# Zeros first, some loads on another queue, and all instruction orders searched anew: recurrent attention and squared-ReLU layers on one core

## The chip, the cores and the metric

The kernel runs on one core of one Trainium2 chip. The metric is the device time of one execution in microseconds (us). The engines are TensorE (PE; its weight loads are listed as PEld), VectorE (DVE), ScalarE (ACT), GpSimd (POOL) and SyncE (SP), which only issues DMAs here. POOL issues DMAs as well, on a queue of its own. In the profile's rows SPq stands for SP as it issues.

## The reference

```python
def _attn_ref(q, k, v, alpha):            # batch 4, heads 8, sequence 768, head size 48, float32
    for t in range(S):
        state = alpha[:, :, t, :, None] * state + np.einsum('bhd,bhe->bhde', k[:, :, t], v[:, :, t])
        y[:, :, t] = np.einsum('bhd,bhde->bhe', q[:, :, t], state)

def _moe_ref(x, w_in, w_out):             # x: 3072 x 384, w_in: 384 x 2048, w_out: 2048 x 384
    h = x @ w_in
    r = np.maximum(h, 0.0)
    return (r * r) @ w_out
```

x is y with batch and sequence as rows and all heads side by side as columns. The inputs are float32; the kernel computes its matmuls in bfloat16.

## The kernel before, in words

The sequence is cut into 12 units of 256 tokens (3 stretches of 768 by 4 batches; `units`). A unit g goes through five stages:

- **Loads** (`load`, L529): alpha, k, q, v of the unit: `lda3`, `ldk3`, `ldq3`, `ldv3` for unit 3. Unit 0 and those from 3 on go through SP's queue. Units 1 and 2 and the weights (`win0` to `win2`, `wout0`, `wout1`, function `weight`, L503) go through POOL's queue, in the order of the list `QUEUE` (L389). A table `AFTER` (L1095) makes a load wait until another has landed: win1 waits for k0, a2 for win1, wout0 for win2, wout1 for k2, the loads of unit 3 for wout0, those of unit 4 for q3.
- **Front** (`front`, L709; `front_by_heads` for unit 0, L549): logs of alpha on ACT (`ln`, `lm`), cumulative sums as matmuls with triangular matrices (`m1`, `m1i`, `m1s`), exponentials on ACT (`ei`, `ea`, `es`), products on POOL or DVE (`pr`, `bk`, `aq`), scaled keys and queries on DVE (`ekm`, `eqm`), and v as bfloat16 (`vc`). Then both are transposed: on PE for units 0 to 2 (`tr0_1` for the keys of unit 1, `tr1_1` for its queries; unit 0 has four, the second digit is the half of the heads), with an eviction after each (`et`), and by two transposing DMAs from SP for units 3 to 11 (also called `tr0_g`, `tr1_g`).
- **Scores and output** (`scores`, L904; `output`, L942): score tiles on PE (`p0_g`; unit 0 has `p0_0` and `p1_0`), masked out of PSUM by DVE (`mk0`, `mk1`), the output matmuls `y`, the state (`kv`, `sa`, `sc`, `sd`), the eviction of y (`xe`), and its transpose (`xt`): on PE for units 0 to 3, with an eviction `xv`, by a transposing DMA from SP for units 4 to 11.
- **First layer** (`first_layer`, L1008): 8 groups `s1_g_0` to `s1_g_7` of 6 matmuls each with 256 columns; each group's ReLU is `re`, its square `sq` (some squares take two groups at once).
- **Second layer** (`second_layer`, L1053): for each half of the rows 4 groups `s2_g_half_0` to `_3` of 4 matmuls each with 384 columns, an eviction `oe` and a store `out`.

Which engine issues what, and in which order, is written out by hand: the table `ORDERS` (L12) lists every operation by name for each engine. Operations without a name have a number: #1 to #13 and #16 to #19 are memsets on DVE (#19 zeroes a buffer `ZERO`, #18 is a part of a mask `OWN`, #6, #7 and #5 clear the scaled keys' and queries' buffers), #14, #15 and #20 to #22 selections on POOL that cut triangles and the identity, #23 a copy on ACT for the causal mask. The class `Program` puts each operation on the engine under which it is listed and works out its semaphore waits. Its `schedule` (L158) also works out planned starts from costs; these starts fix nothing but the order in which waits are derived and where `fill` (L236) puts filler matmuls on PE. A filler multiplies zeros by zeros into a PSUM bank that nobody reads. `fill` is called once (L1127): it puts fillers in PE's planned waits, after the memset of `ZERO` and before the first `s1` group.

In `ORDERS` the memset of `ZERO`, #19, stands last on DVE, behind `oe11_11`. `fill` therefore finds no place, and the kernel before has no filler.

Of the kernel before, what the change touches and what calls it, by code (L numbers as in the profile page):

```python
# [3 lines left out]
ALU = mybir.AluOpType  # L4
# [14 lines left out]
        sq4_7 sq4_6 re5_2 ln8 xe6 oe4_0 ei8 ea8 lm8 re5_5 re5_4 es8 sq5_5 re5_6 re5_7 re6_0 re6_1 sq5_6 ln9 re6_3 lm9
        re6_4 re6_5 ei9 ea9 es9 re6_7 re6_6 sq6_7 oe5_1 re7_1 re7_0 vc9 ln10 sq7_3 re7_5 ei10 lm10 ea10 re7_7 es10  # L20
        sq7_7 oe6_1 re8_1 sq7_5 re8_0 sq7_6 ln11 xe9 lm11 ei11 re8_4 oe7_0 re8_6 re8_5 sq8_6 ea11 re8_7 sq8_1 re9_0
        oe7_1 re9_2 es11 sq8_7 re9_4 oe8_0 xe10 sq9_1 re9_5 oe8_1 sq9_5 sq9_6 re10_1 oe9_0 oe9_1 re10_4 re10_5 re10_6
        re10_7 oe10_0 oe10_1 re11_4 sq11_5 re11_7 oe11_0 oe11_10
    """,
    "dve": """
        #7 #11 #4 #6 #5 #9 #10 #16 #12 #8 #13 #3 #1 #17 ekm0_0 ekm1_0 eqm0_0 #18 eqm1_0 et00_0 et10_0 et11_0 sa0 mk0_0
        mk1_0 ekm1 eqm1 xv0 et1_1 sc0 mk1_1 mk0_1 sa1 #2 re0_3 sq0_1 xe1 pr2 xv1 sq0_5 sc1 re1_0 re1_1 bk2 ekm2 eqm2
        re1_4 et0_2 re1_7 mk1_2 mk0_2 sa2 pr3 sc2 bk3 eqm1_3 ekm3 aq3 eqm0_3 pr4 xe2 sa3 xv2 lb4 ekm4 eqm1_4 eqm0_4
        sc3 re2_2 mk1_3 mk0_3 re2_5 sq2_5 sa4 ekm5 xv3 sc4 lb5 eqm1_5 eqm0_5 mk1_4 mk0_4 re3_2 sq3_3 sa5 re3_5 sc5
        sq3_5 bk6 ekm6 re3_6 lb6 eqm1_6 eqm0_6 mk1_5 mk0_5 re4_2 sq4_1 sa6 re4_4 re4_5 sc6 lb7 oe3_1 ekm7 eqm1_7  # L30
        eqm0_7 mk1_6 mk0_6 sd6 re5_3 sa7 sc7 sq5_3 lb8 ekm8 oe4_1 eqm1_8 eqm0_8 mk1_7 mk0_7 sq5_7 sq6_1 re6_2 xe7
        oe5_0 sa8 lb9 ekm9 eqm1_9 eqm0_9 mk1_8 mk0_8 sq7_1 pr10 re7_3 re7_2 xe8 sa9 oe6_0 re7_4 bk10 ekm10 lb10 mk0_9
        re7_6 eqm1_10 eqm0_10 mk1_9 pr11 sd7 re8_3 re8_2 sq8_3 sa10 lb11 ekm11 sq8_5 mk0_10 eqm1_11 eqm0_11 re9_1
        mk1_10 re9_3 sa11 re9_7 mk0_11 re9_6 mk1_11 re10_0 xe11 re10_2 re10_3 sq10_3 sq10_5 sq10_7 re11_0 re11_1
        re11_2 re11_3 re11_5 re11_6 sq11_6 sq11_7 oe11_11 #19
# [56 lines left out]
class Program:  # L92
# [10 lines left out]
    SWITCH = 95  # L103
# [54 lines left out]
    def schedule(self):  # L158
# [35 lines left out]
        while True:  # L194
# [5 lines left out]
            if heads and (event is None or min(heads)[0] <= event):  # L200
# [958 lines left out]
```

## Time and profile before

| | |
|---|---|
| median of 3 runs | 175.3 us (174.58 to 176.03) |
| the profiled execution | 173.93 us |
| span of its profile | 172.2 us |
| first s1 group of unit 0 starts | 18.19 us into the span |
| DMA | 33.37 MB, mean 194 GB/s |

The columns of the timeline are start, duration, engine, line, operation, out<-in, shape and count; in brackets stands how long the engine had been idle and what ended that. In the windows each engine has its busy time and number of instructions in the stretch. Durations of matmuls are modelled with their pipeline's end, so consecutive ones overlap; the distance between two starts is the pace. The tables of DMA issues give KB of one and the time from issue to landing. The chain is the work that ended last, followed back from the end.

### The profile page before, as it was taken

To read this page: it belongs to the slowest core of one execution; us is meant where nothing else is said; L and a number is where in the kernel's file an instruction comes from. 1 tells how busy PE (TensorE), PEld (TensorE's weight loads), DVE (VectorE), ACT (ScalarE), POOL (GpSimd) and SP (SyncE) were. 2 spreads that over 40 slices of the span, in tenths; PEclk is the share of its full clock that TensorE was granted. 3 is DMA by queue.
4 is the path that set the end of the run, shared out by engine and by line. 5 is a ranking of instruction groups with operands and counts; after the bars stand their busy time and mean duration, and the time that the engine had idled before them with its cause. 6 is when DMAs were issued, how large, how long until landed. Compare 5 with 4: busy or idle time off the path is not lost.

```text
span 172.2 us, 5038 instructions
## 1 busy us (share of the span) xinstructions
PE 160.9 (93%) x2200; PEld 127.6 (74%) x2200; DVE 117.2 (68%) x186; ACT 104.5 (61%) x190; POOL 64.6 (37%) x65
## 2 busy tenths in 40 slices
PE   0696999999999999999999999999999999999994
PEld 0564799756788877887877887878777877687773
DVE  4478889768977787769566848799517709355241
ACT  2837478767677866466785578377668454152240
POOL 4947214910286554481640466001012122403700
PEclk9999999999999999999999999999999999999999
DMA  5999999999997999999999999999983672220012
GB/s 139 346 256 244 291 276 212 204 272 297 159 240 183 292 221 179 221 222 251 205 221 293 219 197 243 162 286 317 183 209 115 90 84 93 48 93 0 24 71 91
DMA packets 71559, 33.37 MB, mean 194 GB/s; under 512 B 67568, under 2 KB 68592, under 8 KB 71536
## 3 DMA queue, kind: packets, MB, share of 16 engines
q1 hardware_dynamic: 69024, 26.75, 70.4%
q0 software_dynamic: 2512, 6.29, 15.4%
q8 instruction: 17, 0.28, 0.7%
q14 instruction: 6, 0.05, 0.1%
HBM read 25.17 MB, written 4.72 MB: 174 GB/s over the span
## 4 chain that ended last, share of the span: by engine, by line
PE 90%; DVE 3%; ACT 2%; DMA 2%; issue 1%; DVEq 0%; ACTq 0%
PE psWH L1029 36%; PE psO L1070 33%; PE psX L925 3%; PE psZ L796 2%; PE psX L828 2%; DMA raw<-in_alpha_dram 2%; PE psX L817 2%; PE psWH L1070 2%; PE psX L997 2%; PE psZ L925 1%; PE psWH L669 1%; DVE pm L936 1%; PE psO L1029 1%; PE psX L864 1%; PE psX L971 1%
## 5 line engine op out<-in xcount | busy, mean ns | idle before, releaser
L1029 PE MATMUL psWH<-xt,win 128*128 128x256 bf16 x552 | 71.0, 274 | 0.2 <-ACT rr L1037 0.2
L1070 PE MATMUL psO<-wout,gt 128*128 128x384 bf16 x352 | 66.3, 326 | 0.0
L1029 PEld LDWEIGHTS psWH<-xt,win 128*128 128x128 bf16 x552 | 61.4, 129 | 5.3 <-DVE xt L983 0.6
L1070 PEld LDWEIGHTS psO<-wout,gt 128*128 128x128 bf16 x352 | 33.4, 98 | 17.5 <-DVE gt L1047 0.5
L1037 ACT ACTIVATE rr<-psWH 128x512 bf16<-128x512 f32 x58 | 33.9, 595 | 15.4 <-PE psWH L1029 14.5
L1050 POOL TENSOR_TENSOR gt<-rr 128x1024 bf16<-128x1024 bf16 (+1 forms) x17 | 28.0, 1654 | 37.4 <-ACT rr L1037 20.8
L1039 DVE TENSOR_SCALAR rr<-psWH 128x512 bf16<-128x512 f32 x34 | 23.4, 690 | 19.5 <-PE psWH L1029 19.0
L1051 ACT ACTIVATE gt<-rr 128x512 bf16<-128x512 bf16 (+1 forms) x26 | 21.1, 824 | 5.8 <-DVE rr L1039 5.8
L1077 ACT ACTIVATE osb<-psO 128x384 f32<-128x384 f32 x18 | 8.8, 490 | 17.0 <-PE psO L1070 16.8
L936 DVE TENSOR_TENSOR pm<-psZ,caus 128x1024 bf16<-128x1024 f32 x12 | 14.6, 1220 | 3.1 <-PE psZ L925 3.1
L726 POOL CAST vbf<-raw 128x768 bf16<-128x768 f32 x8 | 6.7, 832 | 24.6 <-DMA raw<-in_v_dram 24.6
L936 DVE TENSOR_TENSOR pm<-psX,caus 128x1024 bf16<-128x1024 f32 x12 | 14.6, 1216 | 0.5 <-PE psZ L925 0.5
L1047 DVE TENSOR_TENSOR gt<-rr 128x1024 bf16<-128x1024 bf16 (+1 forms) x17 | 10.6, 625 | 2.9 <-ACT rr L1037 2.4
L687 POOL TENSOR_TENSOR ek<-ek,raw 128x384 f32<-128x384 f32 x6 | 6.5, 1082 | 15.8 <-ACT ek L680 15.8
L731 DVE TENSOR_TENSOR qks<-raw,eq 128x384 bf16<-128x384 f32 x18 | 9.4, 553 | 2.6 <-DMA raw<-in_q_dram 1.8
L736 DVE TENSOR_TENSOR qks<-raw,ek 128x768 bf16<-128x768 f32 x11 | 10.5, 955 | 0.5 <-POOL ek L687 0.4
L704 DVE TENSOR_TENSOR la<-psWH,la 128x384 f32<-128x384 f32 x8 | 4.4, 553 | 7.9 <-ACT eq L682 6.5
L661 ACT ACTIVATE lab<-prd 128x384 bf16<-128x384 f32 x10 | 5.2, 522 | 4.1 <-POOL prd L660 2.4
L956 ACT ACTIVATE xbf<-psX 128x768 bf16<-128x768 f32 x7 | 5.7, 810 | 3.3 <-PE psX L817 3.0
L660 POOL TENSOR_TENSOR prd<-raw 128x384 f32<-128x384 f32 x5 | 5.2, 1040 | 4.9 <-DMA raw<-in_alpha_dram 4.9
L680 ACT ACTIVATE ek<-psWH 128x384 f32<-128x384 f32 x10 | 4.9, 490 | 3.0 <-PE psWH L672 2.2
L958 DVE CAST xbf<-psX 128x768 bf16<-128x768 f32 x5 | 4.8, 954 | 2.0 <-PE psX L817 1.3
(128 smaller groups left out, 183.7 us busy)
## 6 DMA issues: line engine op xcount, KB each, us to landing
out_dram<-osb SPq DMA_DIRECT2D x11, 384.0 KB, 4.0
raw<-in_alpha_dram SPq DMA_DIRECT2D x10, 384.0 KB, 4.5
raw<-in_k_dram SPq DMA_DIRECT2D x10, 384.0 KB, 4.6
raw<-in_q_dram SPq DMA_DIRECT2D x10, 384.0 KB, 4.8
raw<-in_v_dram SPq DMA_DIRECT2D x10, 384.0 KB, 4.9
wout<-in_moe_w_out_dram POOLq DMA_DIRECT2D x2, 768.0 KB, 8.4
raw<-in_alpha_dram POOLq DMA_DIRECT2D x2, 384.0 KB, 6.5
raw<-in_k_dram POOLq DMA_DIRECT2D x2, 384.0 KB, 7.2
```

Source lines behind the costliest of these rows:

```text
L731: add("dve", lambda e, j=j, dst=dst: e.tensor_tensor(dst, RAW[r][:, 2, :, j, :].rearrange("p (n x) d -> p n x d", x=2), EQ[la][:, j].rearr ...
L736: add("dve", lambda e, a=a, E=E: e.tensor_tensor(QKS[qs][:, a, :, :, 0:D], RAW[r][:, 1 + a].rearrange("p h j d -> p j h d"), E[la][:].rear ...
L925: ins = pe.matmul(psT[64 * c:64 * c + 64, rr_, o:o + 128], keys, mov)
L936: add("dve", lambda e, hf=hf, psT=psT: e.tensor_tensor(PM[pm][:, hf].rearrange("p r n j t -> p (r n) (j t)"), psT[:, :, :].rearrange("p r ...
L1029: ins = pe.matmul(psF[:, i * T:(i + 1) * T], WIN[:, kk, hidden(fj)], mov, start=(kk == 0), stop=(kk == KT - 1))
L1037: add("act", lambda e, psF=psF, rr=rr: e.activation(rr, psF, AF.Relu), act_ns(512), pu + 600, reads=[keyF], writes=[("rr", rb, half)], nam ...
L1039: alts={"dve": (lambda e, psF=psF, rr=rr: e.tensor_scalar(rr, psF, 0.0, None, ALU.max), dve_ns(512))})
L1047: add("dve", lambda e, dst=dst, sq=sq: e.tensor_tensor(dst, sq, sq, ALU.mult), 148 + k * 267, pu + 1200, reads=[("rr", rb, h) for h in ran ...
L1050: alts={"pool": (lambda e, dst=dst, sq=sq: e.tensor_tensor(dst, sq, sq, ALU.mult), 200 + k * 840), "act": (lambda e, dst=dst, sq=sq: e.act ...
L1051: "act": (lambda e, dst=dst, sq=sq: e.activation(dst, sq, AF.Square), act_ns(k * 512))})
L1070: ins = pe.matmul(psS, GT[gt][:, fj, j, :], WOUT[:, fj, :], start=(fj == 0), stop=(fj == FT - 1))
L1077: add("act", lambda e, j=j, psS=psS: e.activation(OSB[ob][:, j], psS, AF.Copy), act_ns(DM), ps_ + 700, reads=[keyS], writes=[("osb", ob, j ...
```

## The change

Five things are edited, and one of them, the orders, reaches every engine.

1. #19, the memset of `ZERO`, stands first on DVE.
2. The function `fill` and its call are taken out. Instead 24 fillers stand in PE's order by name (`fill512_0` has 512 columns, `fill256_6` has 256), all ahead of the first s1 group: 0 to 6 before the first cumulative sums of unit 0, 7 after them, 8 to 10 after `tr00_0`, 11 to 17 between `m11` and `y0`, 18 and 19 between `tr0_1` and `tr1_1`, 20 to 23 between `xt0` and `p0_1`.
3. The loads of units 1 to 3 may stand on SP's or on POOL's queue (`EITHER`). Two do change: `ldv1` goes to SP, right behind unit 0's loads, and `ldk3` to POOL, behind `sq0_6`.
4. Costs in the planner are changed: memsets, POOL's products, the issue of weight loads, PE's switches between tile shapes (`ENTER`), PE's first 9 us (`COLD`), and how POOL and DVE hold each other up (`OVERLAP`). They change no instruction by themselves.
5. All five orders are other ones. 38 operations move from DVE to ACT and 37 from ACT to DVE, 8 from POOL to ACT and 8 to DVE, 8 from DVE and 7 from ACT to POOL. The computation and the shapes of all operations are as before.

The beginnings of the orders, the tail of DVE's, and the code:

```diff
 ORDERS = {
     "act": """
-        table ln0_0 ln1_0 ei0_0 #23 ei1_0 ea0_0 ec0_0 ea1_0 vc0 et01_0 ec1_0 ln1 ei1 ea1 xe0 et0_1 ec1 re0_2 re0_0
+        table #23 ln0_0 ln1_0 ei0_0 ei1_0 ea0_0 ea1_0 et00_0 vc0 ec0_0 ec1_0 ln1 ei1 ea1 xe0 et1_1 ec1 vc1 re0_2 re0_0
...
     "dve": """
-        #7 #11 #4 #6 #5 #9 #10 #16 #12 #8 #13 #3 #1 #17 ekm0_0 ekm1_0 eqm0_0 #18 eqm1_0 et00_0 et10_0 et11_0 sa0 mk0_0
-        mk1_0 ekm1 eqm1 xv0 et1_1 sc0 mk1_1 mk0_1 sa1 #2 re0_3 sq0_1 xe1 pr2 xv1 sq0_5 sc1 re1_0 re1_1 bk2 ekm2 eqm2
-        re1_4 et0_2 re1_7 mk1_2 mk0_2 sa2 pr3 sc2 bk3 eqm1_3 ekm3 aq3 eqm0_3 pr4 xe2 sa3 xv2 lb4 ekm4 eqm1_4 eqm0_4
...
-        re11_2 re11_3 re11_5 re11_6 sq11_6 sq11_7 oe11_11 #19
+        #19 #6 #11 #8 #12 #1 #10 #7 #9 #5 #2 #16 #17 #13 #3 ekm0_0 ekm1_0 eqm0_0 eqm1_0 et10_0 #18 et01_0 et11_0 sa0
+        mk1_0 mk0_0 ekm1 eqm1 et0_1 xv0 sc0 mk1_1 mk0_1 sa1 sq0_1 sq0_3 xe1 pr2 sc1 xv1 re0_7 re1_0 ekm2 re1_3 sq0_7
+        eqm2 et0_2 et1_2 #4 sq1_7 mk1_2 pr3 mk0_2 sa2 sc2 ekm3 eqm1_3 aq3 pr4 eqm0_3 sd2 oe0_1 xv2 lb4 ekm4 sc3 eqm0_4
...
     "pe": """
-        m10_0 m11_0 tr00_0 tr10_0 tr01_0 tr11_0 kv0 p0_0 p1_0 m11 y0 tr0_1 xt0 tr1_1 p0_1 s1_0_2 s1_0_0 s1_0_1 kv1
-        s1_0_3 y1 s1_0_5 s1_0_4 s1_0_6 xt1 s1_0_7 m1s2 m1i2 s1_1_0 s1_1_1 s1_1_2 s1_1_3 s1_1_4 s1_1_5 s1_1_6 tr0_2
...
+        fill512_0 fill512_1 fill512_2 fill512_3 fill512_4 fill512_5 fill256_6 m10_0 m11_0 fill512_7 tr00_0 fill512_8
+        fill512_9 fill512_10 tr10_0 tr01_0 tr11_0 kv0 p1_0 p0_0 m11 fill512_11 fill512_12 fill512_13 fill512_14
+        fill512_15 fill512_16 fill256_17 y0 tr0_1 fill512_18 fill256_19 tr1_1 xt0 fill512_20 fill512_21 fill512_22
+        fill256_23 p0_1 s1_0_2 s1_0_0 s1_0_1 kv1 s1_0_3 y1 s1_0_4 s1_0_5 s1_0_6 xt1 s1_0_7 m1i2 m1s2 s1_1_0 s1_1_1
...
     "pool": """
-        #22 #15 #21 #14 #20 lda1 ldk1 ldq1 win1 win0 ldv1 win2 lda2 ldq2 ldk2 ldv2 vc1 wout0 wout1 aq2 sq1_3 sd1 sd0
-        vc2 sd2 bk4 sq2_1 pr5 vc4 sd3 bk5 sq2_7 sq3_1 sd4 pr6 sq3_7 sq3_6 vc6 sd5 pr7 sq4_3 bk7 vc7 pr8 sq5_1 bk8 vc8
...
+        #20 #21 #22 #15 #14 lda1 ldk1 ldq1 win1 win0 win2 lda2 ldk2 ldq2 ldv2 wout0 wout1 sd1 bk2 aq2 sd0 vc2 sq0_6
+        ldk3 sq1_6 bk3 vc4 bk4 pr5 sd3 sq2_5 sq2_6 vc5 sq3_1 sd4 sq3_7 vc6 pr7 sd5 sq4_3 sq4_7 pr8 vc7 sq5_1 bk8 vc8
...
     "sp": """
-        lda0 ldk0 ldq0 ldv0 lda3 ldq3 ldk3 ldv3 lda4 ldk4 ldv4 ldq4 tr0_3 tr1_3 lda5 ldk5 tr0_4 tr1_4 out0_1 ldq5 ldv5
...
+        lda0 ldk0 ldq0 ldv0 ldv1 lda3 ldq3 ldv3 lda4 ldk4 ldv4 ldq4 tr1_3 tr0_3 lda5 ldk5 tr0_4 tr1_4 out1_1 ldq5
...
+    EITHER = (1, 2, 3)
...
-    zero = add("dve", fill(ZERO[:], 0.0), 300, -3e6, writes=[("zero",)])
+    add("dve", fill(ZERO[:], 0.0), 300, -3e6, writes=[("zero",)])
...
+            go = lambda e, dst=dst, src=src: e.dma_start(dst, src)
+            load_op[name] = add(ring, go, cost, at,
+                writes=[key], name=f"ld{name}", dma=f"{nm}{r}", lag=1230 if ring == "sp" else 1180,
+                alts={"sp": (go, 600), "pool": (go, 930)} if g in EITHER else None,
                 after=gate(name, g) + ([named(f"{BEHIND[nm]}{g - 1}")] if g >= 5 else []))
...
+    for name in ORDERS["pe"].split():
+        if name.startswith("fill"):
+            n = int(name[4:7])
+            add("pe", lambda pe, n=n: pe.matmul(psO[:, 0:n], ZERO[:, 0:128], ZERO[:, 0:n], skip_group_check=True),
+                216 if n == 512 else 109, 0, reads=[("zero",)], name=name)
     pr.schedule()
-    pr.fill(lambda n: lambda pe: pe.matmul(psO[:, 0:n], ZERO[:, 0:128], ZERO[:, 0:n], skip_group_check=True),
-            ((512, 216, 420), (256, 109, 250)), min(o.start for o in pr.order["pe"] if o.name.startswith("s1_")), zero, 4600)
     pr.place()
```

More of the change, by code (lines that the diff above doesn't have):

```diff
@@ L19 @@
[L19 to L23, printed above, removed]
+        table #23 ln0_0 ln1_0 ei0_0 ei1_0 ea0_0 ea1_0 et00_0 vc0 ec0_0 ec1_0 ln1 ei1 ea1 xe0 et1_1 ec1 vc1 re0_2 re0_0
@@ L32 @@
[L32 to L35, printed above, removed]
+        #19 #6 #11 #8 #12 #1 #10 #7 #9 #5 #2 #16 #17 #13 #3 ekm0_0 ekm1_0 eqm0_0 eqm1_0 et10_0 #18 et01_0 et11_0 sa0
@@ L55 @@
+        s2_11_0_3 s2_11_1_0 s2_11_1_1
     """,
     "pool": """
-        #22 #15 #21 #14 #20 lda1 ldk1 ldq1 win1 win0 ldv1 win2 lda2 ldq2 ldk2 ldv2 vc1 wout0 wout1 aq2 sq1_3 sd1 sd0
-        vc2 sd2 bk4 sq2_1 pr5 vc4 sd3 bk5 sq2_7 sq3_1 sd4 pr6 sq3_7 sq3_6 vc6 sd5 pr7 sq4_3 bk7 vc7 pr8 sq5_1 bk8 vc8
-        pr9 sq6_3 bk9 sq6_6 sq6_5 vc10 bk11 vc11 sq9_3 sq9_7 sq10_1 sq10_6 sq11_1 sq11_3
+        #20 #21 #22 #15 #14 lda1 ldk1 ldq1 win1 win0 win2 lda2 ldk2 ldq2 ldv2 wout0 wout1 sd1 bk2 aq2 sd0 vc2 sq0_6
```

125 lines of the change are left out of this document (55 added, 70 removed).

## The prediction, made before the changed kernel ran

> **What bounds the kernel now.** I read the page from the top: busy shares, the chain that ended last, then stages, then what TensorE (PE) waited for, then the first 18 us instruction by instruction.
>
> ```profile
> span 172.2 us, 5038 instructions
> PE 160.9 (93%) x2200; PEld 127.6 (74%) x2200; DVE 117.2 (68%) x186; ACT 104.5 (61%) x190; POOL 64.6 (37%) x65
> PEclk9999999999999999999999999999999999999999
> DMA  5999999999997999999999999999983672220012
> PE 90%; DVE 3%; ACT 2%; DMA 2%; issue 1%; DVEq 0%; ACTq 0%
> ```
>
> The chain is 90% PE and no other engine comes near. The stages say where PE is not busy:
>
> ```profile
> core 0: us, PE busy (x) PEld busy (x) DVE busy (x) ACT busy (x) POOL busy (x), PEclk, DMA share, GB/s
> 4.90:18.25 13.35, 9.79 (x187) 7.55 (x188) 9.61 (x16) 8.09 (x16) 9.82 (x12) 1.00 1.13 275
> 58.00:98.00 40.00, 39.84 (x618) 31.78 (x607) 31.21 (x47) 26.30 (x50) 18.26 (x16) 1.00 1.10 228
> PE psWH L1029 <- ACT rr L1037: 0.2, 1, 0.2
> PE psX L925 <- issue: 0.2, 1, 0.2
> 102.79 1.31 PE psWH L1029 x12
> ```
>
> The two lines with arrows are all that PE waited for from 18 to 171 us: 0.4 us. The last, from the chain, gives the pace: two groups of six matmuls in 1.31, 0.65 each. Behind 18 us a new order has next to nothing to win and can only add waits. What can shrink is the start:
>
> ```profile
> 0.93 0.27 DVE L456 MEMSET qks<- 128x256 uint32 x1 [0.93 <-PEq L1144]
> 4.35 0.94 ACT L561 ACTIVATE laf<-raw 128x384 bf16<-128x384 f32 x2 [2.26 <-DMA raw<-in_alpha_dram]
> 4.93 0.34 PE L567 MATMUL psX<-laf,linc 128*128 128x192 bf16 x1 [4.93 <-ACT laf L561]
> 5.22 0.37 PE L569 MATMUL psX<-laf,linc 128*128 128x192 bf16 x1
> 5.38 0.37 PE L570 MATMUL psX<-laf,lstr 128*128 128x192 bf16 x1
> 6.26 0.40 ACT L485 ACTIVATE caus<-caus 64x256 bf16<-64x256 bf16 x1
> 6.29 0.29 PE L573 MATMUL psX<-ones,laf 128*128 128x2 bf16 x4
> 6.62 0.49 ACT L582 ACTIVATE ek<-psX 128x384 f32<-128x384 f32 x1
> 7.01 0.61 PE L609 MATMUL psZ<-ident,qks 128*128 128x128 bf16 x4 [0.43 <-DVE qks L597]
> 7.62 0.55 DVE L597 TENSOR_TENSOR qks<-raw,eq 128x384 bf16<-128x384 f32 x1
> 8.22 0.61 PE L609 MATMUL psZ<-ident,qks 128*128 128x128 bf16 x4 [0.61 <-DVE qks L597]
> 8.30 0.56 DVE L597 TENSOR_TENSOR qks<-raw,eq 128x384 bf16<-128x384 f32 x1
> 9.26 1.03 PE L609 MATMUL psZ<-ident,qks 128*128 128x128 bf16 x8 [0.42 <-DVE kqt L616]
> 11.67 1.23 DVE L936 TENSOR_TENSOR pm<-psX,caus 128x1024 bf16<-128x1024 f32 x1
> 12.26 0.33 PE L634 MATMUL psWH<-laf,linc 128*128 128x384 bf16 x1
> 12.42 0.33 PE L635 MATMUL psWH<-laf,linc 128*128 128x384 bf16 x1
> 13.97 0.96 DVE L736 TENSOR_TENSOR qks<-raw,ek 128x768 bf16<-128x768 f32 x1
> 14.99 0.62 PE L759 MATMUL psZ<-ident,qks 128*128 128x128 bf16 x8
> 15.70 1.02 ACT L768 ACTIVATE kqt<-psZ 128x1024 bf16<-128x1024 bf16 x1
> 17.61 0.42 PE L925 MATMUL psX<-kqt 64*64 64x128 bf16 x16 [0.80 <-DVE kqt L766]
> 18.19 0.84 PE L1029 MATMUL psO<-xt,win 128*128 128x256 bf16 x6
> ```
>
> The page grants full clock throughout, yet the starts tell another story: 192 columns every 0.16 us at 5.2 to 5.4, 384 columns in the same 0.16 us at 12.3. PE runs at half speed until about 12.2. Eight transposes take 1.03 us before that and 0.62 after: 0.41 dearer. The dense work begins at 18.19; what leads there is alpha's landing (4.3), logs, exponentials, scaled k and q, transposes, the two masked score tiles (11.67 on), unit 1's scaled k and q (13.97 on), its transposes, p0_1 at 17.61.
>
> **The change, part by part.**
>
> *Zeros first.* In the kernel before, the zeros' memset is VectorE's last instruction, so `fill` found no room and PE issues no filler. Now it comes first, at 0.93, and 24 fillers are written into PE's order. The memset writes 256 words as the row at 0.93 does: 0.27 us on DVE, hidden, because its memsets end near 3.3 and its first real work waits for the exponentials at 6.4; if that cover were gone, 0.27 us of delay. Fillers 0 to 6 run from 1.25: at half speed 512 columns take 0.43 us (192 in 0.16), so six and a half end near 4.05, ahead of 4.93. Filler 7 (6.4 to 6.8) ends before 7.01. Fillers 8 to 10 follow tr00_0, from 7.45; cold they end at 8.73 and hold tr10_0 (8.22 before) by 0.5, warm (0.216 each) they end at 8.10 and hold nothing. Those after m11 (1.4 us warm) end some 0.2 past the point where y0 could start; those behind tr0_1 and xt0 lie in waits.
>
> *When the clock rises.* In this trace it rose 2.9 us after PE became dense at 9.26. With fillers PE is dense from 1.25, idle from 4.05 to 4.93, dense again from there: 4.93 + 2.9 = 7.8, or one gap later, 8.7, against 12.2.
> [...]
>
> *The start's path.* ACT's copy #23 (6.26) goes ahead of the logs, where ACT waits for alpha; it wins nothing, since the exponential behind it started at 6.62, just as the matmuls of 6.29 ended. OWN's memset #18 leaves the place before eqm1_0, which stood 0.68 behind eqm0_0 instead of the usual 0.48: 0.2 won. et00_0 goes to ACT and frees DVE. Then, rise at 8.7: tr10_0 8.73, tr11_0 9.64 (before 9.7), p1_0 10.5 (before 10.97), first mask 11.03 (11.67), ekm1 13.33 (13.97), tr1_1 15.2, et1_1 now on ACT (1.02 as at 15.70) 15.85 to 16.87, p0_1 16.9, dense work 17.5: 0.7 won. Rise at 7.8: tr10_0 starts 0.43 sooner and the chain behind it with it: 1.15. I take 0.9. Bounds: 0.1, if the clock rises no earlier and the cold fillers still stand in the way; 1.3, if it rises before 4.93 and the log matmuls are quick too: win0, landing up to 17.6 (below), then holds s1_0_0, the second group, which began near 18.9.
>
> *Loads on the other queue.*
>
> ```profile
> 7.40 1.51 POOL L513 DMA_DIRECT2D win<-in_moe_w_in_dram  x2
> 8.89 0.91 POOL L545 DMA_DIRECT2D raw<-in_v_dram  x1
> raw<-in_v_dram POOLq DMA_DIRECT2D x1, 384.0 KB, 8.7
> win<-in_moe_w_in_dram POOLq DMA_DIRECT2D x1, 384.0 KB, 7.7
> 25.69 0.58 POOL L513 DMA_DIRECT2D wout<-in_moe_w_out_dram  x1 [3.55 <-DMA raw<-in_k_dram]
> wout<-in_moe_w_out_dram POOLq DMA_DIRECT2D x1, 768.0 KB, 8.2
> raw<-in_k_dram POOLq DMA_DIRECT2D x1, 384.0 KB, 9.7
> xt<-xbf SPq DMA_TRANSPOSE x8, 4.4
> ```
>
> v1 leaves POOL's queue, where it stood between win0 (second of the two at 7.40, issued 8.15 and landed 7.7 later, 15.85) and win2; SP issues it at k0's landing, near 5.4. The DMA engines are nine tenths busy from 4.3 on, so its 1.75 us (8.89 + 8.7 = 17.6, less 15.85) are taken from what then lands later: win0 up to 17.6. s1_0_0 asks for it at about 18. Hidden, with 0.4 us to spare; each tenth beyond counts. k3 leaves SP and goes behind POOL's sq0_6; on that queue it stands behind wout1 (25.69 + 8.2 = 33.9). ekm3 asks for it near 38.8. I take nothing for either; bounds 0 and +2.4 (below).
>
> *The new orders.* 38 operations go from DVE to ACT and 37 back, 16 and 15 between POOL and those two: no engine's sum moves by more than a few us, and the busiest, DVE, has a third idle. Their cover is PE's queue of dense groups (0.65 us each). The distances hold: scores to output at least 2.6 us of PE work (2.8 before), for two masks of 1.2; output to its first s1 at least 5.4 us (6.3; unit 9), for an eviction of about 1 and a transposing load of 4.4 in the median. Thinner by a group in places: I take +0.3 us in all, between -0.3 (PE waited only 0.4) and +1.5. The tail after the last s1 is the same.
>
> **Sum.** The profiled execution took 173.93 us. 173.93 - 0.9 + 0.3 = 173.3. It stands 1.4 below the median of the runs, 175.3 (174.58 to 176.03). Part of that I put down to runs whose clock rose a stretch later: two sets of transposes and scores at half speed on the path, 2 x 0.41, estimated from the rows above. The fillers take that away, so I add 0.6 and not 1.4: **173.9**.
>
> **The rivals.**
> (1) The gain is eaten in the middle: a handful of waits of 0.2 to 0.5 us where distances got thinner. For it: PE had no slack of its own. Against: none up to 40 us when I follow the order by the rows. 173.9 + 1.1 = 175.0.
> (2) Slower: k3 comes late. Loads on POOL's queue landed up to 9.7 us after issue; from 31.4 that is 41.1, 2.4 us after ekm3 asks. ekm3, eqm0_3, both transposing loads and p0_3 follow, and PE stands. 173.9 + 2.4 = 176.3, and 177 and more if the waits of a second unit add to it. It decides once k3 lands later than about 40. Against: the 9.7 was spent behind win2; behind wout1 it should land near 36.5.
> (3) The clock rises before the first log matmuls, and every step of the start profits: 173.9 - 0.4 and the runs' excess gone, -0.8: 172.7.
> (4) The fillers do nothing for the clock: the start wins 0.1 and the runs keep their excess: 173.93 - 0.1 + 0.3 + 1.4 = 175.5; it shares the chance of (1).
>
> **How the numbers follow.** Forecast 0.54, in its own range 172.9 to 174.7; (1) with (4) 0.17; (2) 0.19; (3) 0.10. A measurement of this kernel tells about 1% from no change, that is 173.55 and 177.05. The forecast lies close to the lower bound and splits 0.33 faster, 0.21 same; (1) and (4) 0.16 same, 0.01 slower; (2) 0.04 same, 0.15 slower; (3) 0.10 faster. Faster 0.43, same 0.41, slower 0.16. The range leaves out the outer half of (3) and of (2): 172.4 to 176.5.
>
> **What would show it.** Fillers on psO from 1.25 and transposes of 0.62 per eight from about 8; tr10_0 at 8.2 to 8.8; first mask near 10.6 to 11; the first psO<-xt,win group at 17.0 to 17.5; PE waits of about 0.7 us after it; the last group then ends as much earlier. I am wrong if the transposes at 9 still take 1.03, if PE waits on kqt near 47 us, on win before 19, or on xt anywhere for over 0.5.

## The result, and the profile after

| | median, us | runs |
|---|---|---|
| before | 175.66 (174.58 to 178.66) | 6 |
| after | 180.12 (179.33 to 182.07) | 6 |

The ratio is 1.026, 95% interval 1.021 to 1.032: slower. The forecast was 173.9, the range 172.4 to 176.5. Runs of one kernel scatter by 1 to 3%; medians here are of all runs, every ratio leaves out runs in a disturbed state, and e6 and e14 have too few others for a ratio. The execution profiled before took 173.93 us, 1.7 below that median: profile against profile the change costs 6.2 us, median against median 4.5.

The page of the changed kernel (180.14 us in the profiled run), the same parts as before:

```profile
span 178.4 us, 5088 instructions
PE 165.9 (93%) x2222; PEld 128.5 (72%) x2224; DVE 118.8 (67%) x185; ACT 105.7 (59%) x192; POOL 62.1 (35%) x64
PEclk9999999999999999999999999999999999999999
DMA  5999999999899899989998999995996692040022
PE 47%; DMA 34%; SPq 6%; DVE 6%; ACT 3%; issue 2%; POOL 2%; DVEq 0%
```

PE's share is still 93%, and that line alone would tell nothing: part of the 165.9 us are fillers. What changed is the chain that ended last. PE held 90% of it, now 47%, and DMA holds 34%. The stage that the prediction took as full, and what PE waited for from 17.5 us to the end:

```profile
58.00:98.00 40.00, 36.69 (x531) 28.77 (x529) 30.96 (x43) 24.82 (x47) 15.86 (x14) 1.00 1.05 208
```

```profile
engine line waited for: us in total, times, longest us
PE psWH L1011 <- DMA xt<-xbf: 3.1, 3, 1.8
PE psO L1052 <- ACT osb L1059: 1.9, 2, 1.6
PE psX L799 <- POOL vbf L708: 1.0, 1, 1.0
PE psWH L651 <- ACT lab L643: 0.5, 1, 0.5
PE psX L907 <- DVE qks L713: 0.4, 1, 0.4
```

PE was busy for 36.69 of these 40 us, with 531 instructions, where it had been busy for 39.84 with 618. The five lines add up to 6.9 us; the same list of the kernel before had two lines and 0.4 us. The start, in PE's timeline, did what was forecast:

```profile
1.26 2.95 PE L1111 MATMUL psO<-zero 128*128 128x512 bf16 x7 [1.26 <-DVE zero L436]
6.26 0.38 PE L1111 MATMUL psO<-zero 128*128 128x512 bf16 x1
6.84 0.40 PE L591 MATMUL psZ<-ident,qks 128*128 128x128 bf16 x4 [0.20 <-DVE qks L579]
7.07 0.81 PE L1111 MATMUL psO<-zero 128*128 128x512 bf16 x3
8.05 0.62 PE L591 MATMUL psZ<-ident,qks 128*128 128x128 bf16 x8 [0.17 <-DVE qks L579]
16.90 0.85 PE L1011 MATMUL psO<-xt,win 128*128 128x256 bf16 x6
```

Fillers run from 1.26, the transposes at 8.05 take 0.62 instead of 1.03, and the first s1 group starts at 16.90 instead of 18.19: 1.29 us won. Of this 0.95 are left at p0_4 and nothing at y4. Starts of PE's operations in the profiled runs (us; e4, e12 and e15 are variants of the changed kernel, below). The first s1, p0_4, y8 and the last group have the same work ahead of them in both orders, fillers apart. In the new one p0_3 stands one group of 0.65 us earlier, y4 and y6 two later, y9 two earlier:

| | before | after | e4 | e12 | e15 |
|---|---|---|---|---|---|
| first s1 | 18.19 | 16.90 | 18.81 | 17.73 | 17.10 |
| p0_3 | 48.89 | 47.67 | 49.15 | 47.39 | 48.28 |
| p0_4 | 57.57 | 56.62 | 58.10 | 56.34 | 57.24 |
| y4 | 61.51 | 63.66 | 64.28 | 62.62 | 62.98 |
| y6 | 85.05 | 88.85 | 88.50 | 86.93 | 87.73 |
| y8 | 108.64 | 111.10 | 110.76 | 109.54 | 110.15 |
| y9 | 121.75 | 125.81 | 124.34 | 125.46 | 123.29 |
| s2_11_1_1, the last group | 168.92 | 175.13 | 173.13 | 175.14 | 172.56 |

The last group is 6.21 us late though the first was 1.29 early: 7.5 us were lost between. 6.5 of them are the difference of the two lists of waits. Counted from the starts instead, PE's operations that came 0.3 us or more behind its pace lost 8.5 us behind 17 us, for 0.7 before.

The longest waits can be followed to their places. First the out stores, SP's timeline, then the line of ACT that waits for them:

```profile
47.32 5.21 SPq L729 DMA_TRANSPOSE kqt<-qks  x2
52.58 1.39 SPq L1068 DMA_DIRECT2D out_dram<-osb  x1
54.02 0.43 SPq L525 DMA_DIRECT2D raw<-in_q_dram  x1
54.49 0.80 SPq L1068 DMA_DIRECT2D out_dram<-osb  x1
```

```profile
60.40 0.49 ACT L1059 ACTIVATE osb<-psO 128x384 f32<-128x384 f32 x1 [2.18 <-DMA out_dram<-osb]
```

The orders say who is who: at 52.58 out1_1, at 54.02 q5, at 54.49 out0_1. oe2_0 needs the buffer that out0_1 empties, and waited 2.18 us for its landing; PE's s2_2_1_0 waited 1.78 behind it. The kernel before issued out0_1 first:

```profile
52.76 0.58 SPq L1086 DMA_DIRECT2D out_dram<-osb  x1
53.78 0.37 SPq L545 DMA_DIRECT2D raw<-in_q_dram  x1
```

Then the transposing load xt8:

```profile
107.62 3.47 SPq L729 DMA_TRANSPOSE kqt<-qks  x2
111.14 1.38 SPq L525 DMA_DIRECT2D raw<-in_k_dram  x1
112.56 0.62 SPq L1068 DMA_DIRECT2D out_dram<-osb  x1
115.25 0.37 SPq L525 DMA_DIRECT2D raw<-in_v_dram  x1
115.66 0.58 SPq L525 DMA_DIRECT2D raw<-in_q_dram  x1
116.29 2.33 SPq L959 DMA_TRANSPOSE xt<-xbf  x1
```

SP stands idle from 113.18 to 115.25: v10 waits for tr0_9 to land, and q10 and xt8 stand behind it. What xt8 transposes was there at 113.2. It left 3.1 us later, and s1_8_1 waited 1.97 us. The third:

```profile
85.52 1.01 POOL L642 TENSOR_TENSOR prd<-raw 128x384 f32<-128x384 f32 x1 [3.18 <-DMA raw<-in_alpha_dram]
87.97 0.82 POOL L708 CAST vbf<-raw 128x768 bf16<-128x768 f32 x1 [1.45 <-DMA raw<-in_v_dram]
```

v7 stands behind a8 on SP, which waits for q7 to land, and left at 81.93. On POOL vc7 stands behind pr8, but pr8 was through at 86.53 and vc7 began at 87.97, when v7 had landed: here SP's place alone decided. y6 waited 1.21 us for vc7.

### The profile page after: what moved, and what is told of

Same layout as the page of the kernel before. It is cut to its first block, busy times and chain, and to the rows that moved or that the text cites. A ratio compares the mean times of both kernels' runs of the same rounds, so it can differ in the third digit from the quotient of the medians.

```text
span 178.4 us, 5088 instructions
## 1 busy us (share of the span) xinstructions
PE 165.9 (93%) x2222; PEld 128.5 (72%) x2224; DVE 118.8 (67%) x185; ACT 105.7 (59%) x192; POOL 62.1 (35%) x64
## 4 chain that ended last, share of the span: by engine, by line
PE 47%; DMA 34%; SPq 6%; DVE 6%; ACT 3%; issue 2%; POOL 2%; DVEq 0%
PE psWH L1011 18%; PE psO L1052 15%; DMA raw<-in_q_dram 12%; DMA xt<-xbf 9%; DMA kqt<-qks 5%; DMA raw<-in_alpha_dram 4%; SPq L729 4%; DMA raw<-in_v_dram 3%; DVE qks L713 2%; SPq L525 2%; PE psX L979 1%; DVE pm L918 1%; PE psX L907 1%; PE psWH L1052 1%; PE psZ L741 1%
## 5 line engine op out<-in xcount | busy, mean ns | idle before, releaser
L1019 ACT ACTIVATE rr<-psWH 128x512 bf16<-128x512 f32 x67 | 39.3, 594 | 26.4 <-PE psWH L1011 25.8
L1032 POOL TENSOR_TENSOR gt<-rr 128x1024 bf16<-128x1024 bf16 (+1 forms) x17 | 26.0, 1530 | 32.7 <-DVE rr L1021 23.5
L1021 DVE TENSOR_SCALAR rr<-psWH 128x512 bf16<-128x512 f32 x25 | 17.1, 689 | 15.4 <-PE psWH L1011 14.7
L1033 ACT ACTIVATE gt<-rr 128x1024 bf16<-128x1024 bf16 (+1 forms) x23 | 20.4, 905 | 0.3
L1059 ACT ACTIVATE osb<-psO 128x384 f32<-128x384 f32 x16 | 7.8, 488 | 15.9 <-PE psO L1052 12.1
L713 DVE TENSOR_TENSOR qks<-raw,eq 128x384 bf16<-128x384 f32 x18 | 10.5, 606 | 6.4 <-DMA raw<-in_q_dram 6.4
L1029 DVE TENSOR_TENSOR gt<-rr 128x1024 bf16<-128x1024 bf16 (+1 forms) x20 | 12.1, 606 | 3.6 <-ACT rr L1019 3.5
L940 DVE CAST xbf<-psX 128x768 bf16<-128x768 f32 x7 | 6.7, 954 | 2.9 <-PE psX L799 2.9
L1111 PE MATMUL psO<-zero 128*128 128x512 bf16 (+1 forms) x22 | 6.7, 434 | 1.4 <-DVE zero L436 1.3
L1061 DVE COPY osb<-psO 128x384 f32<-128x384 f32 x6 | 3.3, 556 | 5.4 <-PE psO L1052 3.5
```

The source lines that it names most:

```text
L713: add("dve", lambda e, j=j, dst=dst: e.tensor_tensor(dst, RAW[r][:, 2, :, j, :].rearrange("p (n x) d -> p n x d", x=2), EQ[la][:, j].rearr ...
L1019: add("act", lambda e, psF=psF, rr=rr: e.activation(rr, psF, AF.Relu), act_ns(512), pu + 600, reads=[keyF], writes=[("rr", rb, half)], nam ...
L1021: alts={"dve": (lambda e, psF=psF, rr=rr: e.tensor_scalar(rr, psF, 0.0, None, ALU.max), dve_ns(512))})
L1029: add("dve", lambda e, dst=dst, sq=sq: e.tensor_tensor(dst, sq, sq, ALU.mult), 148 + k * 267, pu + 1200, reads=[("rr", rb, h) for h in ran ...
L1032: alts={"pool": (lambda e, dst=dst, sq=sq: e.tensor_tensor(dst, sq, sq, ALU.mult), 200 + k * 840), "act": (lambda e, dst=dst, sq=sq: e.act ...
L1033: "act": (lambda e, dst=dst, sq=sq: e.activation(dst, sq, AF.Square), act_ns(k * 512))})
```

## The experiments

Theory A after reading the two traces: the new order on SP's queue loses the time. Rivals: the fillers or the other four orders do it; the loads' own pace does.

**e1, e2, e3, e4: the parts apart.** e1 is the kernel before with change 1 and 2 alone in its orders (its code outside the orders is the changed kernel's, planner costs included, and so it is in e5 and e6):

```diff
-dve: #7 #11 #4 ... oe11_11 #19
+dve: #19 #7 #11 #4 ... oe11_11
+pe: the 24 fillers at the same operations
```

> All orders and queues of the kernel before, with the zeros' memset first and the 24 fillers at the same places in PE's order. If the fillers raise the clock early and that shortens the start by itself, the dense work begins 0.6 to 1.1 us sooner (17.1 to 17.6 instead of 18.19) and nothing is lost behind it: 174.6 to 175.1 us against 175.7. If the start's 1.29 us came from the new order instead (copy, evictions on ScalarE, OWN's memset), this kernel stays at 175.7 and may lose 0.2 where fillers stand in the way.

178.48 us, ratio 1.019 (1.010 to 1.028): a miss. The start won 0.39 us, and then one wait took 3 us. VectorE and GpSimd near it, and PE's clock and busy time (windows of PE: length, busy, clock, DMA, GB/s):

```profile
58.45 1.89 POOL L1032 TENSOR_TENSOR gt<-rr 128x1024 bf16<-128x1024 bf16 x1 [2.12 <-ACT rr L1019]
58.51 3.35 DVE L713 TENSOR_TENSOR qks<-raw,eq 128x384 bf16<-128x384 f32 x2 [1.88 <-DMA raw<-in_q_dram]
61.78 1.21 DVE L918 TENSOR_TENSOR pm<-psZ,caus 128x1024 bf16<-128x1024 f32 x1
64.18 0.19 PE L799 MATMUL psX<-sbd,kqt 64*128 64x48 bf16 x1 [2.99 <-DVE pm L918]
```

```profile
62.00:64.00 2.00, 0.00 (x0) 1.00 0.46 71
64.00:66.00 2.00, 1.82 (x66) 0.63 0.77 121
66.00:68.00 2.00, 2.00 (x11) 0.52 2.11 209
68.00:70.00 2.00, 2.00 (x19) 1.00 0.44 98
```

GpSimd's product sq3_1 began at 58.45, VectorE's pair eqm1_5, eqm0_5 0.06 us later, and the pair took 3.35 us instead of 1.03 (one alone takes 0.55). The masks of unit 4 stand behind it on VectorE, y4 behind the masks. When PE came back after 3 us, its granted clock had fallen to 0.63 and 0.52 for the next 4 us. From these shares I estimate (0.37 + 0.48) x 2 = 1.7 us more; by the starts it was 1.5: against the kernel before, y4 came 2.67 us later and p0_5 4.20. There the same stretch reads

```profile
58.84 1.89 POOL L1050 TENSOR_TENSOR gt<-rr 128x1024 bf16<-128x1024 bf16 x1 [2.12 <-ACT rr L1037]
57.88 1.03 DVE L731 TENSOR_TENSOR qks<-raw,eq 128x384 bf16<-128x384 f32 x2 [0.87 <-DMA raw<-in_q_dram]
58.83 1.22 DVE L936 TENSOR_TENSOR pm<-psZ,caus 128x1024 bf16<-128x1024 f32 x1
```

The pair was through by 58.91. The mask at 58.83 beside the product took 1.22 us, as the 24 masks of the kernel before do in the mean; it reads psZ, the pair reads raw and eq. In e1 the product came 0.39 us earlier, as the whole of PE's work did, and q5, for which the pair waits, landed 0.63 later (58.49 for 57.86): together 1 us, and the order of the two turned round. The second of the pair (1.18 us) ran beside GpSimd's next product, sd4, from 60.30 on. Shown are these times, 3.35 for 1.03, and which came first; by what the product holds the pair up is not shown.

e2 is the changed kernel with SP's order of the kernel before, e3 the reverse (v1 and k3 stay on the queue that each kernel has them on):

```diff
-sp: ... tr1_3 tr0_3 lda5 ldk5 tr0_4 tr1_4 out1_1 ldq5 out0_1 ldv5 lda6 tr0_5 tr1_5 ldk6 ...
+sp: ... tr0_3 tr1_3 lda5 ldk5 tr0_4 tr1_4 out0_1 ldq5 ldv5 out1_1 lda6 tr0_5 ldk6 tr1_5 ...
```

> The changed kernel with SP's queue in the order of the kernel before (v1 of unit 1 stays on it, k3 stays on POOL's queue). Theory 1, the loss comes from SP's queue, where a load or store that must wait now stands ahead of one that is needed: the waits for transposes, stores and v behind 60 us (about 6 us of PE's time) go, the start's gain stays: 173.5 to 175. Theory 2, the loss comes from the new orders of the compute engines, which evict and multiply later: it stays at 178.5 or more. Theory 3, k3 behind the weights on POOL's queue makes everything behind it late: it stays at 179 to 180.

180.07 us, ratio 1.027 (1.018 to 1.036): nothing came back. Its longest waits are others, 2.3 us for a transposing load (kqt) and 1.7 in two for xt, and the granted clock fell behind the first (0.72 and 0.50 in two windows of 2 us).

> The kernel before with SP's queue in the order of the changed kernel (v1 and k3 stay where before has them). Theory 1 (SP's order costs): 179 to 182, with PE waiting for transposing loads near 110 to 135 us. Theories 2 and 3: within 1 us of 175.7.

181.26 us, ratio 1.028 (1.014 to 1.041), which rests on two runs, 178.82 and 180.96. So SP's new order alone, put into the kernel before, costs about as much as the whole change, and SP's old order alone wins nothing back in the changed kernel: theory A, that SP's order by itself is to blame, fell. The two runs agree with an order of SP that fits only the other orders with which it was made.

e4 is the changed kernel without fillers and with the zeros last.

```diff
-dve: #19 #6 #11 ... oe11_11
+dve: #6 #11 ... oe11_11 #19
-pe: fill512_0 ... fill256_23 (24 operations)
```

> The changed kernel without the 24 fillers and with the zeros last again. If the fillers carry the start's gain, the dense work begins near 17.5 to 17.9 instead of 16.9. If the loads pace the middle, the end moves by less than 0.4 us (180.0 to 180.5); if PE paces it, the end moves by the same 0.6 to 1.0 as the start (180.7 to 181.1).

177.41 us, ratio 1.014 (1.006 to 1.021). It starts its dense work 1.9 us later than the changed kernel (18.81) and ends 2.0 us earlier; its waits behind 18.5 us add up to 3.2 us instead of 6.9. The loads of unit 3 leave at the same time in all three (a3 at 30.0 before, 29.4 after, 29.1 in e4), q5 at 53.8, 54.0 and 55.2: the loads do not start earlier when PE does. That an earlier PE meets them too soon can account for 1.9 us of waits; why e4 gains 2 us beyond that stays open.

Theory B, from e1: VectorE's products held up by GpSimd's make the waits. Theory C: ready work stands behind a waiting operation on an in-order queue. Rival D: the loads set a pace, and what is mended at one place is lost at the next.

**e5 (theory B).** e1 with sq3_1 moved:

```diff
-pool: ... sq2_7 sq3_1 sd4 pr6 ...
+pool: ... sq2_7 sd4 pr6 ...
+dve: ... sq3_3 sq3_1 sa5 ...
```

> e1_fillers_alone (before's orders, zeros first, 24 fillers: 178.48 us) with one operation moved: sq3_1, a product of 128x1024 with 1.89 us, goes from GpSimd to VectorE, behind sq3_3. Theory 'GpSimd holds VectorE up': in e1 this product began at 58.45, 0.06 us ahead of VectorE's eqm1_5, and the two eqm products, 0.55 us each elsewhere, took 2.25 and 1.18; the masks of unit 4 stand behind them, TensorE idled 3.0 us at y4 and had half its clock for some 3.4 us after that. With the product away: both eqm at 0.55 to 0.6, the wait at y4 under 0.7, no fall of the clock, 174.5 to 175.5 us. Rival 'the loads set the pace': the wait at y4 comes from q5, which lands at 58.5 whatever GpSimd does; the wait shrinks by less than half and comes back at the next unit, 177 to 178.5 us.

175.45 us, ratio 1.004 (1.000 to 1.008). VectorE and PE at the same place:

```profile
58.66 1.03 DVE L713 TENSOR_TENSOR qks<-raw,eq 128x384 bf16<-128x384 f32 x2 [1.78 <-DMA raw<-in_q_dram]
62.01 0.19 PE L799 MATMUL psX<-sbd,kqt 64*128 64x48 bf16 x1 [0.56 <-DVE pm L918]
```

The pair is back at 1.03, the wait at 0.56, the clock stays at 1.00. One operation moved off GpSimd gives back the 3 us that e1 lost. q5 landed as late as in e1 (58.6 for 58.5), so a late q5 alone does not make this wait; it only let the product be first.

**e6: the changed kernel's start, the old middle.**

```diff
 act, dve, pool, pe, sp: the changed kernel's orders up to vc1, sa1, wout1, p0_1 and ldv1
+...: then e5's orders
```

> e5 with the changed kernel's start on every engine: all five orders are the changed kernel's up to the first s1 group (with vc1 on ScalarE and ldv1 on SP), and those of the kernel before behind it, sq3_1 on VectorE as in e5. The first s1 group then starts at about 16.9 instead of 18.2. If the start's gain is carried through wherever no wait stands in its way, 173.8 to 174.5 us. If the loads set the pace (the loads of unit 3 are issued at about 30 us in all kernels, q5 lands at 58 to 59 in all), the 1.3 us are used up by waits between 45 and 75 us, and the time is 175 to 176.5 us or, where such a wait is over 2 us and the clock falls, 177 and more.

Four runs, 173.12, 176.87, 176.88 and 177.09 us. The profiled one, of 176.87, started its dense work at 18.05, because its clock rose late (three fillers from 7.35 on took 1.49 us, 0.81 in the changed kernel; last section). By its time nothing is decided.

**e7, e8: loads two units ahead** (in the changed kernel and in the one before):

```diff
-                after=gate(name, g) + ([named(f"{BEHIND[nm]}{g - 1}")] if g >= 5 else []))
+                after=gate(name, g))
-sp: ... ldq4 tr1_3 tr0_3 lda5 ldk5 tr0_4 tr1_4 ...
+sp: ... ldq4 lda5 ldk5 ldq5 ldv5 tr1_3 tr0_3 lda6 ldk6 ldq6 ldv6 tr0_4 tr1_4 ...
```

> The changed kernel with the loads of units 5 to 11 loosened: the waits of a load for ln, ekm and tr0 of the unit before are taken out (a still waits for the q before it to land), and SP issues the four loads of unit g+2 ahead of the transposes of unit g. Nothing else is moved. If the loop (q lands, eqm, transposes, landing, next q) and the loads behind waiting transposes cause the changed kernel's waits, those at y6, s1_8_1 and for xt go, the waits behind out0_1 and for kqt stay in part: 175.5 to 177.5 us. If instead the loads beside transposes hold these up, transposes take longer from issue to landing than 5.3 us and the time is 180 us or more.

> The same loosening of the loads in the kernel before, nothing else. The kernel before waits behind 18 us for 0.7 us only, so there is next to nothing to win by it: 174.8 to 175.8 us if loads beside transposes cost nothing; 176.5 us and more if they hold the transposes up, or if the other times at which data arrive bring GpSimd's products in front of VectorE's.

185.08 (ratio 1.061, 1.055 to 1.068) and 182.23 us (1.047, 1.039 to 1.055). The edit made a waiting head of its own: a5 waits for q4 to land, and the transposes of unit 3 stood behind it; p0_3 waited 7.5 us in e7 and 5.6 in e8, and the clock fell in both (mean granted clock of the profiled runs 0.972 and 0.981; 1.00 in the changed kernel). Behind it e8 has no wait over 0.6 us. Transposes took 4.8 and 4.5 us in the median from issue to landing, 4.8 before: loads beside them do not hold them up in the median.

**e9, e10, e11.** e9 has the same gates out, and the loads of unit g+2 behind the transposes of unit g; e11 is e6 with that; e10 moves three things on SP's queue of the changed kernel:

```diff
 e9  sp: ... tr1_3 tr0_3 lda5 ldk5 ldq5 ldv5 tr0_4 tr1_4 out1_1 out0_1 lda6 ldk6 ldq6 ldv6 tr0_5 ...
-e10 sp: out1_1 ldq5 out0_1 ldv5 ... xt5 out2_1 lda8 ldv7 ... tr1_9 tr0_9 ldk10 out4_1 ldv10 ldq10 xt8
+e10 sp: out0_1 ldq5 ldv5 out1_1 ... xt5 ldv7 out2_1 lda8 ... tr0_9 tr1_9 ldk10 xt8 ldq10 ldv10 out4_1
```

> The changed kernel with the loads of units 5 to 11 one stage earlier: their waits for ln, ekm and tr0 of the unit before are taken out, and SP issues a, k, q and v of unit g+2 right behind the two transposes of unit g (in e7 they stood ahead of these, and the wait of a5 and a6 for a q to land held up the transposes of unit 3 and 4: 7.5 us at p0_3). out1_1 and out0_1 stay right behind tr1_4. If the loads that wait on SP's queue for a transpose to land (and what stands behind them) cause the changed kernel's waits, then v7, xt8 and q5 come in time: the waits at y6, s1_8_1 and s1_5_0 (3.8 us together) go, and the time is 175 to 177 us. If loads beside transposes are what costs, it is 180 us and more. If GpSimd's products in front of VectorE's are the main cause, the waits move elsewhere and their sum stays at 7 us or more: 179 to 181 us.

180.28 us, ratio 1.035 (1.029 to 1.040). The wait at y6 went, s1_8_1 kept 1.29, and new ones came: 1.59 at p0_4, 1.28 at p0_5, 1.91 at s2_6_1_0 (a store's landing). By the starts these and the smaller ones add up to 8.0 us, so the third branch of the expectation fits, and transposes landed 4.4 us after issue in the median, so the second does not. VectorE's operations that lay beside GpSimd's were lengthened by 7.6 us in sum (counting each that took over 0.25 us more than the median of its line and shape; 2.9 in the changed kernel, none in the one before). That this makes the waits is not shown: e16 below has 3.3 us of it and takes 175.63. Earlier loads alone win nothing: D in its simple form fell.

> The changed kernel with three moves on SP's queue alone: out0_1 ahead of q5 and v5, out1_1 behind them; v7 right behind xt5, ahead of out2_1 and a8; tr0_9 ahead of tr1_9, xt8 ahead of q10 and v10, out4_1 behind them. Theory 'head of SP's queue': these are the causes of the waits at s2_2_1_0 (1.78 us), y6 (1.21) and s1_8_1 (1.97), and each was ready long before its issue. Then some 4 to 5 of the 8.5 us of waits go: 175 to 176.5 us. If each wait only gives way to the next late thing (as with the whole order of SP taken from the kernel before, 180.07), 178 us or more.

185.13 us, ratio 1.058 (1.052 to 1.065). The waits at s2_2_1_0 and s1_8_1 were gone, but out4_1 had been put behind two loads that wait for a transpose: one wait of 5.06 us at s2_6_1_0. The mean granted clock of the profiled run was 0.991, for 1.00 in the changed kernel. The miss shows theory C's price better than the hits.

> e6 (the changed kernel's start, the orders of the kernel before behind it, sq3_1 on VectorE) with the loads of units 5 to 11 one stage earlier as in e9. In e6 the profiled run waited 1.04 us at y4 for the masks behind eqm1_5 (q5 landed at 59.0), 0.71 at y6 and 1.17 at s1_8_1. With q5 at about 51 and each later q some 8 us earlier these go, if the loads' pace is what uses up the start's gain: 172.5 to 174 us. If loads beside transposes cost what they save, 175 to 176.5 us.

175.99 us, ratio 1.011 (1.003 to 1.018): one long wait, 2.43 us, for xt4, which stood behind the transposes of unit 5, a7 and k7.

**e12, e15: the changed kernel with four and with five moves.**

```diff
-sp: ldk10 xt8 ldq10 ldv10 out4_1        (e10)
+sp: ldk10 out4_1 xt8 ldq10 ldv10        (e12, e15)
-pool: pr8 vc7 ... vc10 sq7_1
+pool: vc7 pr8 ... vc10 sq7_1            (e12)
+pool: vc7 pr8 ... sq7_1 vc10            (e15)
```

> e10 with its out4_1 back ahead of xt8 and the loads of unit 10 (in e10 it stood behind these, which wait for tr0_9 to land; oe6_0 then waited for it, 5.06 us at s2_6_1_0, and the clock fell), and one more move: on GpSimd vc7 ahead of pr8, as in the kernel before (pr8 waits for a8, which lands at 85.8; vc7 behind it ends at 87.7, and y6 waited 1.56 us for it). So it is the changed kernel with four moves. Theory 'ready work behind a waiting head': the waits at s2_2_1_0, y6 and s1_8_1 (5.0 us) are gone and nothing else changes: 174.8 to 176.3 us, no fall of the clock. Rival 'each wait gives way to the next late thing': 177.5 us or more.

180.21 us, ratio 1.031 (1.021 to 1.040): the rival's number. The three waits were gone, and PE stood 1.6 us ahead of the changed kernel at y8. Then it lost 3.15 us at s1_8_3. GpSimd and ScalarE there:

```profile
110.55 1.04 POOL L1032 TENSOR_TENSOR gt<-rr 128x512 bf16<-128x512 bf16 x1
120.52 0.97 POOL L708 CAST vbf<-raw 128x768 bf16<-128x768 f32 x1 [8.93 <-DMA raw<-in_v_dram]
121.46 1.89 POOL L1032 TENSOR_TENSOR gt<-rr 128x1024 bf16<-128x1024 bf16 x1
```

```profile
123.38 0.60 ACT L1019 ACTIVATE rr<-psWH 128x512 bf16<-128x512 f32 x1 [4.22 <-POOL gt L1032]
```

GpSimd waited 8.9 us in vc10 for v10 (whose place e10 had put behind q10), sq7_1 stood ready behind it, and ScalarE's re8_1 wanted sq7_1's buffer.

> e12 with one more exchange, on GpSimd: sq7_1 ahead of vc10. In e12 the waits at s2_2_1_0, y6 and s1_8_1 were gone (PE stood 1.6 us ahead of the changed kernel at y8), but s1_8_3 waited 3.15 us: re8_1 on ScalarE wants the buffer that sq7_1 reads, sq7_1 stands behind vc10 on GpSimd, and vc10 waits for v10, which lands at 120.5. If this is again one piece of ready work behind a waiting head, the exchange gives back 3 us and what follows keeps its distance: 176.5 to 177.8 us. If the loads of unit 10 set the pace at this place, the time is lost at y9 or s1_9_1 instead: 179 us and more.

177.82 us, ratio 1.013 (1.008 to 1.018). Exchanging the two gave back 2.4 us, as C had it. Five short moves on two queues, none of which touches an amount of work, take half of the loss away; no single wait over 0.9 us is left, and 3.9 us of small ones.

**e13, e16: the best of both.** e13 is e11 with each xt ahead of the loads; e16 has v5 back behind out0_1.

```diff
-sp: tr1_5 lda7 ldk7 xt4 ldq7 ldv7        (e11, and so for xt5 to xt8)
+sp: tr1_5 xt4 lda7 ldk7 ldq7 ldv7        (e13, e16)
-sp: lda5 ldk5 ldq5 ldv5 tr0_4 tr1_4 out0_1 lda6        (e13)
+sp: lda5 ldk5 ldq5 tr0_4 tr1_4 out0_1 ldv5 lda6        (e16)
```

> e11 (new start, old middle, loads one stage earlier) with each xt on SP's queue ahead of the loads it followed (xt4 stood behind a7, which waits for q6 to land; its one long wait was 2.4 us at s1_4_1 for xt4, issued at 67.0). If that is the last thing that uses up the start's gain: s1_4_1 without a wait over 0.5 us, and 173 to 174 us. If not, the gain goes at another wait: 175 us and more.

> e13 with v5 back behind out0_1, so that only q5 of the loads of unit 5 stands newly ahead of the transposes of unit 4. e13's one long wait was 1.55 us at p0_4 for these transposes, which left later (two more loads ahead of them). If they leave 0.6 us earlier and land a further 0.5 us earlier for having less beside them: a wait of 0.5 to 0.8 us at p0_4 and none over 0.5 us behind it, 173.3 to 174.5 us. If v5 in its new place holds a6 up, a wait of 1 us or more comes elsewhere: 175 us.

174.87 (ratio 0.999, 0.993 to 1.004) and 175.63 us (1.000, 0.996 to 1.004). Both have the changed kernel's start and no wait over 1.6 us; neither beats the kernel before. In e16 the wait at p0_4 went and one of 1.0 us came at p0_6, as the second branch of its expectation has it.

**e14: two of the new places put into the kernel before.**

```diff
-sp: out0_1 ldq5 ldv5 out1_1
+sp: out1_1 ldq5 out0_1 ldv5
-pool: vc7 pr8
+pool: pr8 vc7
```

> The kernel before with two of the changed kernel's orders put in: on SP out1_1 ahead of q5 and out0_1 behind q5; on GpSimd pr8 ahead of vc7. Nothing else. Theory 'ready work behind a waiting head': out0_1 is issued at about 54.4 instead of 52.8, oe2_0 waits for its landing, some 1 to 1.5 us at s2_2_1_0; vc7 starts behind pr8 at about 85.2 instead of 81.8, and y6 waits about 1 us: 176.5 to 177.8 us. If the kernel before has room for this (the waits are hidden by those of the masks at y4), 175 to 175.8 us.

Four runs, 176.09, 179.16, 179.19 and 180.34 us. In the profiled one, of 180.34, GpSimd and VectorE read

```profile
59.41 1.89 POOL L1050 TENSOR_TENSOR gt<-rr 128x1024 bf16<-128x1024 bf16 x1 [1.98 <-ACT rr L1037]
59.77 3.05 DVE L731 TENSOR_TENSOR qks<-raw,eq 128x384 bf16<-128x384 f32 x2 [2.19 <-DMA raw<-in_q_dram]
```

q5, behind out1_1, came later, sq3_1 was first, and y4 waited 2.6 us; s2_2_1_0 waited 0.62 and y6 0.84, less than expected of the two exchanges (1 to 1.5 and 1). In this run an exchange on SP made a collision of e1's kind, so B and C can be links of one chain. It is the longest of the four runs; the shortest, 176.09, left no trace, so what the exchanges cost as a rule stays open.

## Why the prediction was wrong, step by step

- *Zeros first, the clock, the start's path (-0.9, bounds 0.1 to 1.3):* right, 1.29 in the profiled run. Transposes at 8.05 with 0.62, first s1 at 16.90; forecast were 17.0 to 17.5. The time of the rise was not right: four transposes took 0.40 at 6.84 already, where they had taken 0.61, and by the rows the prediction had 7.8 or 8.7. For a rise before 4.93, on which the bound of 1.3 and rival (3) rest, no row of before speaks; of the runs with this start, e13 had one (last section), the changed kernel had not. The size is in part luck: in the eleven profiled runs with this start the first s1 came between 16.59 and 18.06, 17.08 in the median, and 0.18 of the 1.29 is an earlier first log matmul (4.75 for 4.93).
- *Loads on the other queue (0, bounds 0 to +2.4):* right. k3 left at 31.7 and landed at 37.0, before ekm3 asked; PE waited for no win. The slower rival (2) named a late k3; that did not come.
- *The runs' excess (+0.6):* wrong by 0.6; the profiled run after (180.14) is at the median of its runs.
- *The new orders (+0.3, bounds -0.3 to +1.5):* this is the step that failed. "The distances hold" counted PE's work between two of its own operations against the durations of one eviction, two masks, one transposing load. Each supplier, though, stands in its engine's or queue's own order behind others, and these may be waiting. Those queues were not followed past 40 us, and every one of these waits comes later (the first at 41.7); the one at p0_3 is such a case (eqm0_3 stands on VectorE behind pr4, which waited 0.88 us for a4). Measured, profile against profile: +7.5 for +0.3.
- That *"the last group then ends as much earlier"* failed with it. The sum added the start's gain and the orders' price as if each stood alone. Fillers in the old orders cost 1.9% (e1), the new orders without fillers 1.4% (e4), both together 2.6%; e5 and e13 start their dense work 0.86 and 1.60 us earlier than the kernel before and take as long as it. So a part of the 7.5 us is an earlier start that meets the same queues; how much is not shown.
- *"Behind 18 us a new order has next to nothing to win and can only add waits"* held, and so did rival (1)'s mechanism, the gain eaten in the middle. Its size was wrong: not a handful of 0.2 to 0.5, but three of 1.2 to 2.0 and four of 0.5 to 0.9. Both warnings that the prediction gave itself, a wait at p0_3 near 47 (0.57) and one on xt over 0.5 (1.8), came true.

Shown by e1 with e5: GpSimd's product ahead of VectorE's pair at unit 5, and what it costs in e1; one run of e14 shows the same. Shown by e15, with e10 and e12 on the way: pieces of ready work behind waiting heads cost the changed kernel half of its loss. Of its three longest waits none was traced to such a product. The rest, 2.2 us in e15 against the kernel before, is not taken apart, so the cause is shown for about half.

## What to carry to other kernels

When a change writes new orders for several in-order engines and queues, take each operation that waits for a landing and list what stands ready behind it, on DMA queues as on engines; one place cost PE 1.2 to 7.5 us here, and a longest-chain line full of PE says only that the old order had none. Price the order by those places and not by engine sums or by distances on the busiest engine. An order that waits for almost nothing is a fit of all queues to each other: part of another order broke it in e3, and an earlier start in e1, where two operations shifted by 1 us against each other.

## What the runs showed of the hardware

With the same fillers PE does not reach full pace at the same time in every run. In the changed kernel the fillers were at full pace from 7.07 (three in 0.81 us, above). In e16, with the same instructions up to there:

```profile
7.37 1.49 PE L1111 MATMUL psO<-zero 128*128 128x512 bf16 x3
8.65 1.76 PE L591 MATMUL psZ<-ident,qks 128*128 128x128 bf16 x12
```

Three took 1.49 us, and the first s1 group came at 18.06 instead of 16.59 (e13, which has the same start). In e13 the log matmuls were quick from 4.76 on, 192 columns every 0.08 us; in the changed kernel and in e16 they took 0.16. So the start's gain is 0.1 to 1.6 us from run to run of kernels with this start. What sets the time of the rise is not shown.

The fall is as uneven: the granted clock fell behind a wait of 2.3 us in e2 (0.72 and 0.50 in the two windows of 2 us behind it), of 2.6 in e14 (0.61, 0.53) and of 3.0 in e1 (0.63, 0.52). It stayed at 1.00 behind 2.4 us in e11 and behind the 3.15 us in e12, whose windows of PE read

```profile
122.00:124.00 2.00, 0.00 (x0) 1.00 1.08 359
124.00:126.00 2.00, 1.97 (x53) 1.00 0.32 90
```

In e1 the fall cost half as much again as the wait: 1.5 us on top of 3.0.
